# Products as two column tiles of 64 on TensorE: scores, values, denominators and MLP of an attention and MLP kernel

## The chip, the cores and the metric

One Trainium2 chip, one of its cores. The time is the device time of one launch in microseconds, median of several runs; lower is better. The kernel before took 470.49 us (three runs, 470.36 to 472.8).

PE is TensorE, which multiplies; PEld is the part of it that loads weights. ACT is ScalarE, DVE is VectorE, POOL is GpSimd, SP is SyncE, which issues DMAs.

## The reference

Attention with a relative position bias over 8 batches, 8 heads, 576 positions and 64 columns a head, followed by an MLP over the 4608 rows of 512 columns that the attention leaves:

```
scores = q @ k.T / sqrt(64) + bias[bucket(|i - j|), head]
attn   = softmax(scores)
x      = (attn @ v), heads beside one another      # 4608 x 512
h      = x @ w_in                                   # 4608 x 2048
g      = h + sin(alpha * h)**2 / (alpha + 1e-9)
out    = g @ w_out                                  # 4608 x 512
```

Inputs and output are float32; the products are computed in float16 with sums in float32.

## The kernel before, in words

The eight batches t are worked one after another, and each is an attention stage and an MLP-in stage. In an attention stage four head pairs p follow one another; the two heads of a pair are z = 0 and 1. The 576 queries are cut into two windows of 384 and 192 columns (`WIN`).

- **Scores** (`plan_pair`, `qk`, L565): keys x queries. The tile `kz` holds the keys of each head beside 64 zero rows, so that one 128-row product gives the scores of one head. A window of 384 takes nine products, one to a PSUM buffer `sc`; one of 192 also takes nine, all but one of them two to a buffer. ACT turns each buffer into exponentials in `u` (L572), DVE multiplies those near the diagonal by the bias factor (L605, L588).
- **av** (`plan_av`, L631 and L637): for each window two tasks, y = 0 the denominators (weights are ones) and y = 1 the values (weights are v). A task is nine matmuls into one PSUM buffer `av`: first L631 for the last 64 keys of both heads with 128-column weights (`ones2` or `vh`), then L637 eight times with 64-column weights, head 0 to output rows 0 to 63 and head 1 to rows 64 to 127. ACT makes the reciprocal of the denominators (Ln at L653, Exp at L657), and DVE multiplies it in and writes the MLP's input `xT` (L668).
- **MLP-in** (`plan_moe_in`, L693): 512 rows of x to a block, 16 blocks of 128 hidden columns f, four products of 512 columns each into an `sc` buffer; ACT takes the sine (L700), ACT or DVE the square (L707, L709), DVE adds (L714) into the tile `g`.
- **MLP-out** (`plan_mo`, L741): for each 128 rows, 16 products of 512 columns into a `mo` buffer, copied out by DVE or ACT (L473, L471). There are nine blocks: 4608 rows of 512; the last batch has two of them.
- **Start**: `warm` (L388) issues products on zeros; q and k of batches 0 and 1 are turned by transposes on PE (L486, L493), into `mo` buffers that ACT and DVE copy. From batch 2 on, DMA transposes do it.

The order on each engine is not written by hand. Every piece of work is a task with dependencies, a priority and a guessed duration; `Plan.run` simulates the four engines and emits at each step the task that can start first (ties within 0.02 us by priority). MLP-out products are fill: they have the lowest priority, so they go where PE would otherwise stand still, and during the scores of a batch no more than `OFFSET + QUOTA * share` of them are taken. av tasks carry the mark `tiled`, and where the mark of a PE task differs from that of the one before, the planner adds `D_MODE` (0.115 us) to its start. Two `g` tiles are in use in turn, so the MLP-in of block 8 needs the MLP-out of block 6 done.

Of the kernel before, what the change touches and what calls it, by code (L numbers as in the profile page):

```python
# [152 lines left out]


WINDOW = 700
D_MODE = 0.115
WARM_END = 40.0
FILL_GAP = 0.0
QUOTA = 48
# [28 lines left out]
def kernel(  # L188
# [11 lines left out]
    nc = tc.nc  # L200
# [8 lines left out]
    NF = FF // 128  # L209
# [4 lines left out]
    XN = 1536  # L214
# [21 lines left out]
    kzs = [sgl.tile([128, NP, 2 * S], F16, name=f"kz{i}") for i in range(2)]  # L236
# [18 lines left out]
    zz = sgl.tile([128, 512], F16, name="zz")  # L255
# [125 lines left out]
    def clear_v(eng, i):  # L381
        eng.memset(vhs[i][0:64, :, 1, :], 0.0)
        eng.memset(vhs[i][64:128, :, 0, :], 0.0)

    def warm(n):
        x = new_mo()
        for _ in range(n):
            nc.tensor.matmul(out=x, lhsT=zz[:, 0:128], rhs=zz, start=True, stop=True)  # L388

    def cast0(kq, j, eng):  # L390
        n = SN[2 * j]
# [147 lines left out]
    def plan_pair(t, p, kqt, first, gate, ub, band_nb):  # L539

        u = Cell()
        done = {}
        units, head = [], []
        for w in range(2):
            units += [(w, 4, 0)]
            for c in range(0, 4, 1 + w):
                units += [(w, c, 0), (w, c, 1)]
        for i, (w, c, z) in enumerate(units):
            q0, n = WIN[w]
            nc_ = 1 if w == 0 or c == 4 else 2  # L550
            b, sc = Buf("sc"), Cell()

            def qk(e, i=i, w=w, c=c, z=z, q0=q0, n=n, nc_=nc_, sc=sc):
                if i == 0:
                    if p == 0:
                        first()
                        plan.in_qk, plan.used = True, 0
                    u.v = new_u()
                plan.share = (len(units) * p + i + 1) / (NP * len(units))
                if p == NP - 1 and i == len(units) - 1:  # L560
                    plan.in_qk = False
                sc.v = new_sc()
                for y in range(nc_):
                    k0 = 512 if c == 4 else (128 * (c + y), S + 64 + 128 * (c + y))[z]
                    nc.tensor.matmul(  # L565
                        out=sc.v[:, n * y : n * y + n], lhsT=kzs[t % 2][:, p, k0 : k0 + 128],
                        rhs=qTs[t % 2][:, p, q0 : q0 + n], start=True, stop=True,
                    )

            def ex(e, w=w, c=c, z=z, q0=q0, n=n, nc_=nc_, sc=sc):  # L570
                k0 = 8 if c == 4 else 4 * z + c
                nc.scalar.activation(  # L572
                    out=u.v[:, k0 : k0 + nc_, q0 : q0 + n], in_=sc.v[:, 0 : n * nc_],
                    func=AF.Exp, scale=0.125,
                )

            base = PB + 100 * (16 * p + i)
            m = plan.add({"PE": nc_ * t_pe(n)}, qk, kqt, base, after=head, new=[b] + ([ub] if i == 0 else []))
            head = head or [m]
            x = plan.add({"ACT": t_act(n * nc_)}, ex, [m] + gate, base + 20, use=[b, ub])  # L580
            if c == 4:
                if w == 0:
                    done[(w, 4, 0)] = done[(w, 4, 1)] = x
                    continue

                def bh(e):
                    io = u.v[:, 8, 384:576]
                    nc.vector.tensor_tensor(out=io, in0=io, in1=mh[:, p, 0:192], op=ALU.mult)  # L588

                x = plan.add({"DVE": 0.17}, bh, [x] + mh_tasks, base + 10, nb=band_nb, use=[ub])  # L590
                done[(w, 4, 0)] = done[(w, 4, 1)] = x
                continue
            for y in range(nc_):
                done[(w, c + y, z)] = x
            if z == 0:
                continue
            for cc in range(c, c + nc_):
                lo, hi = max(q0, 128 * cc - 128), min(q0 + n, 128 * cc + 256)
                if lo >= hi:
                    continue  # L600

                def bd(e, cc=cc, lo=lo, hi=hi):
                    io = u.v[:, 0:8, lo:hi].rearrange("p (z c) q -> p z c q", z=2)[:, :, cc]
                    x0 = lo - 128 * cc + 128
                    nc.vector.tensor_tensor(  # L605
                        out=io, in0=io, in1=m2[:, 2 * p : 2 * p + 2, x0 : x0 + hi - lo],
                        op=ALU.mult,
                    )

                x = plan.add({"DVE": 0.07 + (hi - lo) / 960.0}, bd,  # L610
                             [done[(w, cc, 0)], done[(w, cc, 1)]], base + 10, nb=band_nb,
                             use=[ub])
                done[(w, cc, 0)] = done[(w, cc, 1)] = x
        return u, done
# [3 lines left out]
    def plan_av(t, p, w, u, ub, done):  # L618

        q0, n = WIN[w]  # L620
        lb, rb = Buf("ln"), Buf("rd")
        bs, avs = [Buf("av"), Buf("av")], [Cell(), Cell()]
        ln, rd = Cell(), Cell()
        base = PB + 100 * (16 * p + 8 * w + 8)
        us = [done[(w, c, z)] for c in range(5) for z in range(2)]
        prev = av_last
        for y in range(2):

            def mm(e, y=y):
                o = avs[y].v = new_av()  # L630
                nc.tensor.matmul(  # L631
                    out=o[:, 0:n], lhsT=vhs[t % 2][:, p] if y else ones2,
                    rhs=u.v[:, 8, q0 : q0 + n], start=True, stop=False,
                )
                for c in range(4):
                    for z in range(2):
                        nc.tensor.matmul(  # L637
                            out=o[64 * z : 64 * z + 64, 0:n],
                            lhsT=vs[t % 2][:, c, 2 * p + z, :] if y else ones,
                            rhs=u.v[:, 4 * z + c, q0 : q0 + n],  # L640
                            start=False, stop=(c == 3),
                        )

            prev = [plan.add({"PE": 5 * t_pe(n)}, mm, us + prev[:], base + AV_PRI + y,
                             nb=T_V0 if t == 0 and y else 0.0, new=[bs[y]], use=[ub])]
            prev[0].tiled = True
            if y:
                av_last[:] = prev
                continue

            def lg(e):
                ln.v = new_ln()
                nc.scalar.activation(out=ln.v[:, 0:n], in_=avs[0].v[:, 0:n], func=AF.Ln)  # L653

            def rc(e):
                rd.v = new_rd()
                nc.scalar.activation(  # L657
                    out=rd.v[:, 0:n], in_=ln.v[:, 0:n], func=AF.Exp, scale=-1.0
                )

            l_ = plan.add({"ACT": t_act(n)}, lg, prev, base + LN_PRI, new=[lb], use=[bs[0]])
            r = plan.add({"ACT": t_act(n) + 0.04}, rc, [l_], base + LN_PRI, new=[rb], use=[lb])

        def ml(e):
            x0 = (S * t + q0) % XN
            for a, m in ((0, min(n, XN - x0)), (min(n, XN - x0), n)):
                if a < m:
                    nc.vector.tensor_tensor(  # L668
                        out=xT[:, p, (x0 + a) % XN : (x0 + a) % XN + m - a],
                        in0=avs[1].v[:, a:m], in1=rd.v[:, a:m], op=ALU.mult,  # L670
                    )

        return r, [plan.add({"DVE": t_dve(n)}, ml, av_last[:] + [r], base - 300,
                            use=[bs[1], rb])]
# [5 lines left out]
    def plan_moe_in(b, tbl):  # L680
# [5 lines left out]
        for f in range(NF):  # L686
# [3 lines left out]
            def mm(e, f=f, h=h):  # L690
                h.v = new_sc()
                for j in range(4):
                    nc.tensor.matmul(  # L693
                        out=h.v, lhsT=w_in16[:, j, 128 * f : 128 * f + 128],
                        rhs=xT[:, j, 512 * b % XN : 512 * b % XN + 512], start=(j == 0), stop=(j == 3),
                    )

            def sn(e, f=f, h=h, s16=s16):
# [34 lines left out]
    def plan_mo(b, a):  # L733

        mb, ob, m = Buf("mo"), Buf("outs"), Cell()
        for f in range(NF):

            def mm(e, f=f):
                if f == 0:
                    m.v = new_mo()  # L740
                nc.tensor.matmul(  # L741
                    out=m.v, lhsT=gcell[b].v[:, f, 128 * a : 128 * a + 128],
                    rhs=w_out16[:, f, :], start=(f == 0), stop=(f == NF - 1),
                )

            mo_last[:] = [plan.add({"PE": t_pe(512)}, mm, mo_last[:] + [gdone[(b, f)]],
                                   500000000 + 4 * b + a, nb=T_WO if b == 0 else 0.0, new=[mb] if f == 0 else [],
                                   use=[gbuf[b]] if f == 0 else [gbuf[b], mb])]
            mo_last[0].fill = True
# [88 lines left out]
```

## Time and profile before

| | |
|---|---|
| three runs, us | 470.49 median (470.36, 470.49, 472.8) |
| the profiled execution, us | 473.36 |
| its span, first to last instruction, us | 471.6 |
| its granted PE clock, mean | 0.993 |
| matmuls on PE | 3073 |
| ACT busy, share of the span | 81% |

The page gives for each engine the time in which at least one instruction of it was running, then the same in 40 slices of the span (a 9 is 90% or more), then groups of instructions by line. A group's row has the count, the busy time, the mean duration of one, and the idle time ahead of it with its cause. A timeline row has the start, the length from first start to last end, and the instructions that it merges. Matmul rows overlap: the next one starts before the one ahead has ended, so the distance between starts is what a product costs, and the duration is not. PEclk is the share of the full clock that PE was granted.

### The profile page before, as it was taken

What the parts mean: (1) busy time and instruction counts of PE and PEld (TensorE: products, weight loads), DVE (VectorE), ACT (ScalarE), POOL (GpSimd) and SP (SyncE); (2) the same over time, 40 slices, a digit from 0 to 9 for tenths busy, and PEclk for the clock granted to TensorE, in tenths of its full rate; (3) what the DMA queues carried; (4) which work ended last, traced back from release to release, by engine and by line L of the source; (5) the groups of instructions that cost most, each with busy time, mean ns of one, the idle gap of its engine ahead of it and who ended that gap; (6) DMA issues with size and microseconds to landing.
All of it is one profiled execution on the core that took longest, in us unless ns stands there. A gap on an engine that the chain in (4) does not pass through costs nothing.

```text
span 471.6 us, 8180 instructions
## 1 busy us (share of the span) xinstructions
PE 452.2 (96%) x3073; PEld 225.6 (48%) x3073; DVE 269.2 (57%) x565; ACT 383.4 (81%) x834; POOL 91.1 (19%) x104
## 2 busy tenths in 40 slices
PE   5688899999999999999999999999999999999996
PEld 2344444554455445554455445544555455544442
DVE  3745496446844585449544764568544954489600
ACT  2769799869988799779987998879887998799611
POOL 7669640007000420025000700040000000000000
PEclk9989899999999999999999999999999999999999
DMA  9699999409900996049901990094101000100021
GB/s 132 172 218 180 185 158 178 87 26 180 159 28 24 117 168 62 24 101 161 108 24 46 177 147 22 24 143 81 46 1 44 2 23 24 46 1 1 22 90 67
DMA packets 144935, 41.28 MB, mean 88 GB/s; under 512 B 132424, under 2 KB 139776, under 8 KB 144896
## 3 DMA queue, kind: packets, MB, share of 16 engines
q0 software_dynamic: 94720, 16.88, 45.2%
q1 hardware_dynamic: 49360, 23.52, 21.8%
q10 hardware_dynamic: 816, 0.36, 0.3%
q8 instruction: 24, 0.39, 0.3%
q14 instruction: 15, 0.12, 0.1%
HBM read 37.56 MB, written 16.52 MB: 115 GB/s over the span
## 4 chain that ended last, share of the span: by engine, by line
PE 60%; ACT 23%; DMA 8%; issue 5%; POOL 2%; DVE 2%; ACTq 0%; POOLq 0%; DVEq 0%
PE mo L741 21%; PE av L637 15%; PE sc L565 12%; PE sc L693 6%; PE av L631 5%; ACT L762 4%; DMA nat_95<-in_q_dram 3%; ACT sq L707 3%; ACT u L572 2%; DMA w_in_79<-in_moe_w_in_dram 2%; DMA w_out_80<-e_dram 1%; POOL m_77 L446 1%; DVE g L714 1%; DMA tabL<-in_bias_table_dram 1%; DMA e_dram<-e_sb 1%
## 5 line engine op out<-in xcount | busy, mean ns | idle before, releaser
L572 ACT ACTIVATE u<-sc 128x384 f16<-128x384 f32 x448 | 173.0, 545 | 3.9 <-PE sc L565 3.8
L741 PE MATMUL mo<-w_out_80,g 128*128 128x512 f16 x576 | 173.5, 379 | 0.0
L693 PE MATMUL sc<-xT,w_in_79 128*128 128x512 f16 x576 | 130.5, 379 | 0.3 <-DVE g L714 0.3
L605 DVE TENSOR_TENSOR u<-u,m_77 128x512 f16<-128x512 f16 (+1 forms) x192 | 73.8, 402 | 73.6 <-ACT u L572 72.0
L714 DVE SCALAR_TENSOR_TENSOR g<-sq,inv_a,sc 128x512 f16<-128x512 f16 x144 | 104.6, 747 | 3.6 <-ACT sq L707 0.6
L693 PEld LDWEIGHTS <-w_in_79 128*128 128x128 f16 x576 | 55.5, 98 | 66.9 <-issue 0.6
L741 PEld LDWEIGHTS <-g 128*128 128x128 f16 x576 | 55.6, 97 | 53.3 <-issue 4.1
L565 PE MATMUL sc<-qT_70,kz_67 128*128 128x384 f16 (+1 forms) x288 | 63.7, 285 | 0.2
L565 PE MATMUL sc<-qT_69,kz_66 128*128 128x384 f16 (+1 forms) x288 | 62.1, 288 | 1.5 <-ACT u L572 0.3
L653 ACT ACTIVATE lnd<-av 128x384 f32<-128x384 f32 x64 | 27.1, 423 | 43.8 <-PE av L637 43.8
L668 DVE TENSOR_TENSOR xT<-av,rd 128x384 f16<-128x384 f32 (+1 forms) x68 | 29.5, 438 | 55.4 <-ACT rd L657 32.5
L637 PE MATMUL av<-u,ones 128*64 128x192 f16 (+1 forms) x512 | 44.2, 295 | 0.0
L565 PEld LDWEIGHTS <-kz_66 128*128 128x128 f16 x288 | 25.9, 98 | 22.1 <-issue 6.1
L565 PEld LDWEIGHTS <-kz_67 128*128 128x128 f16 x288 | 26.7, 97 | 19.8 <-issue 0.8
L335 POOL DMA_DIRECT2D v_72<-in_v_dram x12 | 10.6, 894 | 122.2 <-PE av L637 122.2
L473 DVE COPY outs<-mo 128x512 f32<-128x512 f32 x28 | 19.3, 688 | 18.3 <-PE mo L741 18.3
L657 ACT ACTIVATE rd<-lnd 128x384 f32<-128x384 f32 x64 | 28.3, 442 | 1.2
L637 PEld LDWEIGHTS <-ones 128*64 128x64 f16 x512 | 21.8, 110 | 13.8 <-issue 7.8
L335 POOL DMA_DIRECT2D v_71<-in_v_dram x12 | 10.6, 894 | 86.2 <-PE av L637 86.2
L637 PE MATMUL av<-u,v_71 128*64 128x384 f16 (+1 forms) x256 | 23.1, 304 | 0.0
L637 PE MATMUL av<-u,v_72 128*64 128x384 f16 (+1 forms) x256 | 21.8, 292 | 0.0
L471 ACT ACTIVATE outs<-mo 128x512 f32<-128x512 f32 x8 | 4.8, 597 | 20.6 <-PE mo L741 20.6
(361 smaller groups left out, 396.8 us busy)
## 6 DMA issues: line engine op xcount, KB each, us to landing
out_dram<-outs SPq DMA_DIRECT2D x36, 256.0 KB, 2.0
staged_k<-in_k_dram POOLq DMA_DIRECT2D x6, 576.0 KB, 13.8
staged_q<-in_q_dram POOLq DMA_DIRECT2D x6, 576.0 KB, 15.4
w_out_80<-in_v_dram SPq DMA_DIRECT2D x8, 256.0 KB, 4.3
w_in_79<-in_moe_w_in_dram POOLq DMA_DIRECT2D x4, 512.0 KB, 10.1
w_out_80<-in_moe_w_out_dram POOLq DMA_DIRECT2D x4, 512.0 KB, 10.6
v_71<-in_v_dram POOLq DMA_DIRECT2D x12, 128.0 KB, 4.4
v_72<-in_v_dram POOLq DMA_DIRECT2D x12, 128.0 KB, 4.5
```

The source lines that it names most:

```text
L335: nc.gpsimd.dma_start(out=vs[t % 2][:, c], in_=vp[128 * c : 128 * c + 128],)
L565: nc.tensor.matmul(out=sc.v[:, n * y : n * y + n], lhsT=kzs[t % 2][:, p, k0 : k0 + 128], rhs=qTs[t % 2][:, p, q0 : q0 + n], start=True, st ...
L572: nc.scalar.activation(out=u.v[:, k0 : k0 + nc_, q0 : q0 + n], in_=sc.v[:, 0 : n * nc_], func=AF.Exp, scale=0.125,)
L605: nc.vector.tensor_tensor(out=io, in0=io, in1=m2[:, 2 * p : 2 * p + 2, x0 : x0 + hi - lo], op=ALU.mult,)
L631: nc.tensor.matmul(out=o[:, 0:n], lhsT=vhs[t % 2][:, p] if y else ones2, rhs=u.v[:, 8, q0 : q0 + n], start=True, stop=False,)
L637: nc.tensor.matmul(out=o[64 * z : 64 * z + 64, 0:n], lhsT=vs[t % 2][:, c, 2 * p + z, :] if y else ones, rhs=u.v[:, 4 * z + c, q0 : q0 + n] ...
L653: nc.scalar.activation(out=ln.v[:, 0:n], in_=avs[0].v[:, 0:n], func=AF.Ln)
L657: nc.scalar.activation(out=rd.v[:, 0:n], in_=ln.v[:, 0:n], func=AF.Exp, scale=-1.0)
L668: nc.vector.tensor_tensor(out=xT[:, p, (x0 + a) % XN : (x0 + a) % XN + m - a], in0=avs[1].v[:, a:m], in1=rd.v[:, a:m], op=ALU.mult,)
L693: nc.tensor.matmul(out=h.v, lhsT=w_in16[:, j, 128 * f : 128 * f + 128], rhs=xT[:, j, 512 * b % XN : 512 * b % XN + 512], start=(j == 0), s ...
L714: nc.vector.scalar_tensor_tensor(out=gcell[b].v[:, f, :], in0=sq.v, scalar=inv_a[:, f : f + 1], in1=h.v, op0=ALU.mult, op1=ALU.add,)
L741: nc.tensor.matmul(out=m.v, lhsT=gcell[b].v[:, f, 128 * a : 128 * a + 128], rhs=w_out16[:, f, :], start=(f == 0), stop=(f == NF - 1),)
```

## The change

A helper `mm2` issues each product as two matmuls, one for weight columns 0 to 63 into output rows 0 to 63, and one for columns 64 to 127 into rows 64 to 127, both with the same moving operand. It is used for the warm-up, the scores, the first product of each av task, and both MLP products. The transposes stay, and so does the small product for the bias table. What is computed is the same. The planner's `D_MODE` becomes 0.

```diff
-D_MODE = 0.115
+D_MODE = 0.0
...
+    def mm2(out, lhsT, rhs, start, stop):
+
+        for z in range(2):
+            nc.tensor.matmul(
+                out=out[64 * z : 64 * z + 64], lhsT=lhsT[:, 64 * z : 64 * z + 64], rhs=rhs,
+                start=start, stop=stop,
+            )
+
     def warm(n):
         x = new_mo()
         for _ in range(n):
-            nc.tensor.matmul(out=x, lhsT=zz[:, 0:128], rhs=zz, start=True, stop=True)
+            mm2(x, zz[:, 0:128], zz, True, True)
...
-                    nc.tensor.matmul(
-                        out=sc.v[:, n * y : n * y + n], lhsT=kzs[t % 2][:, p, k0 : k0 + 128],
-                        rhs=qTs[t % 2][:, p, q0 : q0 + n], start=True, stop=True,
+                    mm2(
+                        sc.v[:, n * y : n * y + n], kzs[t % 2][:, p, k0 : k0 + 128],
+                        qTs[t % 2][:, p, q0 : q0 + n], True, True,
                     )
...
-                nc.tensor.matmul(
-                    out=o[:, 0:n], lhsT=vhs[t % 2][:, p] if y else ones2,
-                    rhs=u.v[:, 8, q0 : q0 + n], start=True, stop=False,
+                mm2(
+                    o[:, 0:n],
+                    (vhs[t % 2][:, p] if y else ones2).rearrange("p z d -> p (z d)"),
+                    u.v[:, 8, q0 : q0 + n], True, False,
                 )
...
-                    nc.tensor.matmul(
-                        out=h.v, lhsT=w_in16[:, j, 128 * f : 128 * f + 128],
-                        rhs=xT[:, j, 512 * b % XN : 512 * b % XN + 512], start=(j == 0), stop=(j == 3),
+                    mm2(
+                        h.v, w_in16[:, j, 128 * f : 128 * f + 128],
+                        xT[:, j, 512 * b % XN : 512 * b % XN + 512], j == 0, j == 3,
                     )
...
-                nc.tensor.matmul(
-                    out=m.v, lhsT=gcell[b].v[:, f, 128 * a : 128 * a + 128],
-                    rhs=w_out16[:, f, :], start=(f == 0), stop=(f == NF - 1),
+                mm2(
+                    m.v, gcell[b].v[:, f, 128 * a : 128 * a + 128], w_out16[:, f, :],
+                    f == 0, f == NF - 1,
                 )
```

PE's instructions go from 3073 loads and 3073 matmuls to 4940 each. In the new kernel every one that `mm2` issues has the line of the helper, L388, and L637 is L646, L493 is L501. With `D_MODE` at 0 the planner also sets another order. The 128 av tasks stood in 37 unbroken runs on PE and now stand in 91, most of them one or two tasks with scores between. An attention stage of batches 1 to 7 had 61 to 64 MLP-out products and has 50 to 52; an MLP-in stage had 3 and has 3 to 5; behind the start of the last MLP-in block there were 125 and are 187.

The first place is on PE in the first attention stage with MLP-out products (batch 1), where the first denominators begin; a row is the line, the instruction, output<-inputs and output size. Before:

```order
L741 LDWEIGHTS g
L741 MATMUL mo<-w_out_80,g 128x512
L565 LDWEIGHTS kz_67
L565 MATMUL sc<-qT_70,kz_67 128x384
L631 LDWEIGHTS ones_76
L631 MATMUL av<-u,ones_76 128x384
L637 LDWEIGHTS ones
L637 MATMUL av<-u,ones 64x384
```

and now:

```order
L388 LDWEIGHTS kz_67
L388 MATMUL sc<-qT_70,kz_67 64x192
L388 LDWEIGHTS ones_76
L388 MATMUL av<-u,ones_76 64x384
L388 LDWEIGHTS ones_76
L388 MATMUL av<-u,ones_76 64x384
L646 LDWEIGHTS ones
L646 MATMUL av<-u,ones 64x384
```

The 128-row outputs are gone: scores, the first product of the task and the rest all have 64 rows. The task also comes earlier, behind the last scores of its own head pair instead of behind the first seven of the next.

The second place is on PE at the end of the attention stage of batch 0, around the transposes (of `nat_95`, batch 1's q and k). Before, they follow the last scores, and the last head pair's av tasks follow the second group of twelve:

```order
L565 LDWEIGHTS kz_66
L565 MATMUL sc<-qT_69,kz_66 128x192
L493 LDWEIGHTS nat_95
L493 MATMUL mo<-id_sb,nat_95 64x128
L493 LDWEIGHTS nat_95
L493 MATMUL mo<-id_sb,nat_95 64x128
```

```order
L493 LDWEIGHTS nat_95
L493 MATMUL mo<-id_sb,nat_95 64x32
L631 LDWEIGHTS ones_76
L631 MATMUL av<-u,ones_76 128x384
L637 LDWEIGHTS ones
L637 MATMUL av<-u,ones 64x384
```

and now the first transposes follow the values of the long window:

```order
L646 LDWEIGHTS v_71
L646 MATMUL av<-u,v_71 64x384
L646 LDWEIGHTS v_71
L646 MATMUL av<-u,v_71 64x384
L501 LDWEIGHTS nat_95
L501 MATMUL mo<-id_sb,nat_95 64x128
```

Both av tasks of 384 columns have moved ahead of the transposes; the two of 192 columns now stand behind twelve and behind twenty-four of them.

## The prediction

> **What bounds the kernel now.** I read the busy shares first, then the slices, then stretches of one batch, then single rows.
>
> ```profile
> PE 452.2 (96%) x3073; PEld 225.6 (48%) x3073; DVE 269.2 (57%) x565; ACT 383.4 (81%) x834; POOL 91.1 (19%) x104
> PE   5688899999999999999999999999999999999996
> PEclk9989899999999999999999999999999999999999
> ```
>
> PE is full from the sixth slice on, at its full clock; the first five slices (59 us) are not. Batches 1 to 6 repeat: one stretch from table load to table load, then batch 3 cut into its attention stage and its MLP-in stage.
>
> ```profile
> 175.08:225.71 50.63, 50.48 (x345) 25.60 (x344) 30.06 (x65) 44.36 (x98) 9.24 (x8) 1.00 0.81 92
> 327.06:377.69 50.63, 50.48 (x345) 25.60 (x344) 30.07 (x65) 44.36 (x98) 0.00 (x0) 1.00 0.06 22
> 175.08:208.80 33.72, 33.66 (x261) 17.83 (x259) 15.87 (x41) 27.99 (x71) 0.00 (x0) 1.00 0.40 54
> 208.80:225.71 16.91, 16.82 (x88) 7.77 (x85) 14.19 (x25) 16.38 (x27) 9.24 (x8) 1.00 1.62 166
> ```
>
> Columns: window, its length, busy PE, PEld, DVE, ACT, POOL, granted clock, DMA, GB/s. PE is busy 50.48 of 50.63 us, ACT 44.36. But a matmul row lasts longer than its turn, so busy is not work; the turn is the distance between starts:
>
> ```profile
> 201.33 0.33 PE L565 MATMUL sc<-qT_70,kz_67 128*128 128x384 f16 x1
> 201.49 0.38 PE L741 MATMUL mo<-w_out_80,g 128*128 128x512 f16 x1
> 201.71 0.33 PE L565 MATMUL sc<-qT_70,kz_67 128*128 128x384 f16 x1
> ...
> 202.84 0.25 PE L565 MATMUL sc<-qT_70,kz_67 128*128 128x192 f16 x1
> 202.93 0.38 PE L741 MATMUL mo<-w_out_80,g 128*128 128x512 f16 x1
> ...
> 441.43 26.28 PE L741 MATMUL mo<-w_out_80,g 128*128 128x512 f16 x121
> ```
>
> The 121 products at the end step by (26.28 - 0.38) / 120 = 0.216 us at 512 columns. 384 and 192 columns by proportion give 0.162 and 0.081; the rows show 0.16 and 0.09. Now the av tasks (denominators with ones, values with v):
>
> ```profile
> 188.75 0.34 PE L631 MATMUL av<-u,ones_76 128*128 128x384 f16 x1
> 189.02 0.84 PE L637 MATMUL av<-u,ones 128*64 128x384 f16 x8
> 189.79 0.34 PE L631 MATMUL av<-u,vh_74 128*128 128x384 f16 x1
> 190.06 0.84 PE L637 MATMUL av<-u,v_72 128*64 128x384 f16 x8
> 190.83 0.26 PE L631 MATMUL av<-u,ones_76 128*128 128x192 f16 x1
> 191.02 0.52 PE L637 MATMUL av<-u,ones 128*64 128x192 f16 x8
> 191.47 0.82 PE L565 MATMUL sc<-qT_70,kz_67 128*128 128x384 f16 x4
> ```
>
> A task is one 128-wide product and four pairs of 64-wide ones. Long: 189.79 - 188.75 = 1.04 us where five turns are 0.81. Short: 191.47 - 190.83 = 0.64 where five are 0.41. The excess is 0.23 either way. It splits alike too: 0.11 between the wide product and the first pair (0.27 - 0.16; 0.19 - 0.08), 0.12 over the four pairs (0.77 - 0.65; 0.45 - 0.33). An excess that doesn't grow with the columns is a fixed price of going from wide to narrow and back. The Trainium skill, "TensorEngine Tiling (Array Packing)", Key Properties, says that a change of tiling mode drains the engine; these rows agree.
>
> A whole batch is then 128 MLP products x 0.216 = 27.6, 36 + 36 score products 8.7, sixteen av tasks of five turns 9.7, together 46.0; with 16 x 0.23 = 3.7 it is 49.7 of the 50.63 measured. So 0.9 us a batch is real waiting, and **PE's turns set the time** from batch 1 on.
>
> **The change, part by part.** *The switches.* Everything in batches 1 to 7 becomes 64-wide, so the 0.23 goes 7 x 16 = 112 times. I take 0.225 for rounding: **-25.2 us**. The profiled execution took 473.36 us and PE's span is 471.6; the three runs have a median of 470.49. I sum in differences and apply them to the median, 2.87 below the profiled one.
>
> *The pairs in place of wide products.* 576 score, 128 av, 576 + 576 MLP products: 1856 new pairs. What a new pair costs beyond the old product is not shown at 512, but pairs at 384 and 192 bound it. Of the 0.12 over four pairs the way back to wide should take what the way in takes, 0.11; that leaves 0.01 / 4 = 0.0025 us a pair. If the way back were free it would be 0.03. A pair below the old turn is excluded, since each half streams all columns. I take 0, the nearest to equal ways in and out: **0 us**; ends 0 and +4.6 (1856 x 0.0025), with 0.03 kept for a rival.
>
> ```profile
> L741 PEld LDWEIGHTS <-g 128*128 128x128 f16 x576 | 55.6, 97 | 53.3 <-issue 4.1
> L637 PEld LDWEIGHTS <-ones 128*64 128x64 f16 x512 | 21.8, 110 | 13.8 <-issue 7.8
> ```
>
> A load of half the columns lasts longer, 110 against 97 ns, and there will be two. The eight loads of a short run sum to 0.88 us and the run steps in 0.45, so they lie beside one another and beside products; the cover is the previous pair, and 512 columns give more of it than 192. One rule of the Trainium skill speaks against this change: "TensorE: Matmul & The Clock Gate", Part 3, The mechanism, says that a weight load overlaps running matmuls only where the row group differs, and column tiles share theirs. By that rule no load of a pair would be hidden; the 0.45 us of this trace disagrees with it. If the rule held here all the same, the sum would be that of the third rival below.
>
> *The start.* In batch 0 PE waits for data, and there the order counts:
>
> ```profile
> 45.66 0.58 PE L493 MATMUL mo<-id_sb,nat_95 128*64 128x128 f16 x12
> 46.48 0.30 PE L493 MATMUL mo<-id_sb,nat_95 128*64 128x128 f16 x4 [0.25 <-DMA nat_95<-in_q_dram]
> 47.99 0.58 PE L493 MATMUL mo<-id_sb,nat_95 128*64 128x128 f16 x8 [1.20 <-DMA nat_95<-in_q_dram]
> 48.50 0.44 PE L631 MATMUL av<-u,ones_76 128*128 128x384 f16 x1
> ...
> 50.30 0.50 PE L631 MATMUL av<-u,vh_73 128*128 128x384 f16 x1
> ...
> 52.11 0.26 PE L631 MATMUL av<-u,ones_76 128*128 128x192 f16 x1
> ...
> 55.54 5.35 PE L693 MATMUL sc<-xT,w_in_79 128*128 128x512 f16 x24
> 45.00:50.00 5.00, 3.44 (x39) 1.72 (x36) 1.71 (x5) 3.52 (x9) 5.00 (x5) 0.86 1.14 154
> 50.00:55.00 5.00, 4.35 (x55) 2.24 (x51) 2.20 (x4) 3.09 (x6) 1.56 (x2) 0.80 1.22 201
> ```
>
> 24 transposes of batch 1 stand ahead of the last av tasks, and their data lands at about 48. The two long av tasks then cost 52.11 - 48.50 = 3.6 us, slowed by a clock of 0.86 and 0.80. In the changed order they stand ahead of the transposes, where PE otherwise waits. The gain is at most 3.6 plus the switches of the two short tasks, 0.45; it is nothing if MLP-in 0 starts by another clock. I take **-3.0**, since the first product of MLP-in follows these rows directly; ends 0 and -5. The other batch 0 switches lie beside ACT's exps and the loads and count nothing; without that cover they would be 12 x 0.225 = 2.7, of which the end of -5 has a part.
>
> *What is late next.* With the holes of PE gone, ACT is close. The program order has 50 to 52 output products (L741) in an attention stage instead of 61 to 64, and 187 behind the last batch's second MLP-in start instead of 125. This moves work, and PE loses none by it. But the attention stage becomes 33.72 - 3.6 - 10 x 0.216 = 28.0 us of PE, and ACT is busy 27.99 in it. ACT's real need is a little less, as rows overlap there:
>
> ```profile
> L572 ACT ACTIVATE u<-sc 128x384 f16<-128x384 f32 x448 | 173.0, 545 | 3.9 <-PE sc L565 3.8
> 176.37 1.65 ACT u L572 x4
> ACT lnd L653 <- PE av L637: 5.8, 7, 1.8
> ```
>
> Four exps step by (1.65 - 0.545) / 3 = 0.37 (0.545 is the mean of the first row). The third row, from the waits of this batch, says that ACT stood 5.8 us for av results, which the shorter av tasks also cut. Two engines in program order with the same load trade small waits. Bounds: 0 (all in holes) and 3.0 a batch (half the 5.8 kept on top of 27.99). I take 0.6, near the 0.9 that PE waits now: 7 x 0.6 = **+4.2 us**. The tail (row 441.43) is unchanged: PE alone, 0.216 a product.
>
> Sum: -25.2 + 0 - 3.0 + 4.2 = -24.0. That is 449.4 in the profiled execution's terms and **446.5 us** against the median.
>
> **The rivals.** *ACT takes over* (463 us): the waits of ACT for av stay by half, an attention stage becomes 27.99 + 2.9 = 30.9 instead of 28.0, and 7 x 3.0 = 21 replaces 4.2, which adds 16.8. For it: the equal loads, and a plan whose holes are now all filled. Against: ACT's rows overlap, and it waits for av tasks that get shorter. Anything between 455 and 463 belongs here.
>
> *Pairs cost more than products* (511 us, the slower side): the way back is free and each pair pays 0.03 for its two longer loads. Then only the entries go, 112 x 0.11 = 12.3, and 470.5 - 12.3 - 3.0 + 1856 x 0.03 (55.7) = 511. It decides from 24.0 / 1856 = 13 ns a pair. For it: 110 against 97 ns, twice as many loads, and no pair of 512 columns in this trace. Against: the excess is 0.12 for short and long runs alike, though a short one has half the cover.
>
> *No load is hidden* (651 us): each pair stands for one load of 0.110 us before it streams, and 1856 x 0.110 = 204 comes on top of 446.5. Against: eight such loads, 0.88 us, fit into 0.45. This is what the rule on row groups in the Trainium skill ("TensorE: Matmul & The Clock Gate", Part 3, The mechanism) would do.
>
> *The change does not do what it says* (470 us): the 0.23 comes with each av task for another reason, such as its first weights, and stays. Then only the start moves, and its ends are 0 and -3. Against: the price is the same with ones and with v, going in and coming out.
>
> **How the numbers follow.** Forecast 0.74 (446.5, own range 438.5 to 455), ACT takes over 0.16, no effect 0.04, dearer pairs 0.05, loads not hidden 0.01. Downward: -5 at the start and no new waiting give 446.5 - 2 - 4.2 = 440.3, and the 0.9 a batch that waits now may shrink by some; I end at 438.5. Upward 459 takes dear pairs by 0.0025 (+4.6) and half of the ACT case (+8), and leaves the slower cases out. Faster by over 0.5% (2.35 us, about what a measurement of this kernel can tell from no change): 0.74 + 0.16 = 0.90; within it 0.04; slower 0.05 + 0.01 = 0.06.
>
> **What would show it.** In the profile after, an av task of five pairs of 384 columns should step in 0.81 us and one of 192 in 0.41, without a gap to its neighbours; the products at the end should still step by 0.216 (0.23 or more there is the pair rival). A batch should take 50.63 - 3.6 + 0.6 = 47.6 us, less 1.9 for nine output products that move to the end, so 45.7, with PE waiting 1.5 of them; 48 with waits between PE and ACT is the ACT rival. MLP-in 0 should start at about 52.5 instead of 55.54, and 187 output products should stand around and behind the last MLP-in. Wrong would be a granted clock below 1.00 in batches 1 to 7, or av tasks that keep 1.04.

## The result, and the profile after

The changed kernel takes **447.21 us** (four runs, 445.36 to 447.94) against 471.03 for the kernel before: a ratio of 0.9483, 95% interval 0.9442 to 0.9523. The profiled execution took 446.98 us with a span of 445.2; that of before took 473.36 and 471.6. The busy shares, and PE and its clock in 40 slices, on the page of after:

```profile
PE 426.2 (96%) x4940; PEld 302.8 (68%) x4940; DVE 261.9 (59%) x555; ACT 385.3 (87%) x844; POOL 91.0 (20%) x104
PE   5879999999999999999999999999999999999996
PEclk9999999999999999999999999999999999999999
```

PE has 60% more instructions and is busy 26 us less; ACT's busy time is nearly the same (385.3 against 383.4 us). The granted clock is 0.9 or more in every slice. Batch 3 of after by windows, whole and then its attention and its MLP-in stage, with the columns of the prediction:

```profile
160.58:206.10 45.52, 45.13 (x546) 33.73 (x543) 28.83 (x62) 44.46 (x100) 9.23 (x8) 1.00 0.92 84
160.58:189.35 28.77, 28.38 (x390) 22.62 (x387) 15.06 (x39) 28.13 (x73) 0.00 (x0) 1.00 0.42 51
189.35:206.10 16.75, 16.75 (x160) 11.11 (x157) 13.77 (x24) 16.33 (x27) 9.23 (x8) 1.00 1.78 140
```

A batch has gone from 50.63 to 45.52 us, attention from 33.72 to 28.77. In this window PE issues 119 products of 512 columns, 76 of 384 and 76 of 192 (a pair counted as one), at the prediction's 0.216, 0.162 and 0.081 us a total of 44.2. So 1.3 us is not product time; before it was 50.63 - 46.1 = 4.5, switches included. I call this the **rest** of a batch below. In batches 1 to 6 of after it lies between 0.9 and 1.4. The av tasks of that batch, on PE's timeline of after:

```profile
166.47 0.35 PE L388 MATMUL av<-u,ones_76 128*64 128x384 f16 x2
166.63 0.84 PE L646 MATMUL av<-u,ones 128*64 128x384 f16 x8
167.28 0.36 PE L388 MATMUL av<-u,vh_74 128*64 128x384 f16 x2
...
168.42 0.28 PE L388 MATMUL av<-u,ones_76 128*64 128x192 f16 x2
168.50 0.52 PE L646 MATMUL av<-u,ones 128*64 128x192 f16 x8
168.83 0.68 PE L388 MATMUL sc<-qT_70,kz_67 128*64 128x384 f16 x6
```

A long task steps in 167.28 - 166.47 = 0.81 us (1.04 before), a short one in 168.83 - 168.42 = 0.41 (0.64 before). The 0.23 is gone from both. What the loads show, from the groups of after:

```profile
L646 PEld LDWEIGHTS <-ones 128*64 128x64 f16 x512 | 30.5, 110 | 4.2
```

The same loads as before, 110 ns each, without the 7.8 us of "issue" that stood ahead of them, which fits loads that are not taken ahead across a change of width. The end, by the chain of waits, first of before, then of after:

```profile
441.59 26.13 PE mo L741 x121
...
390.75 13.60 PE mo L388 x126
415.18 26.13 PE mo L388 x242
```

242 halves take the 26.1 us that 121 whole products took. A pair of 512 columns costs what the product cost. The 63 products at 390.75 are those that moved there from the batches.

The start, on PE's timeline of after, then the same windows as in the prediction, and what waited in MLP-in 0:

```profile
43.90 0.36 PE L388 MATMUL av<-u,ones_76 128*64 128x384 f16 x2
...
45.52 0.58 PE L501 MATMUL mo<-id_sb,nat_95 128*64 128x128 f16 x12
...
47.81 0.60 PE L501 MATMUL mo<-id_sb,nat_95 128*64 128x128 f16 x8 [1.00 <-DMA nat_95<-in_q_dram]
...
49.81 5.37 PE L388 MATMUL sc<-xT,w_in_79 128*64 128x512 f16 x48
45.00:50.00 5.00, 3.94 (x80) 3.01 (x77) 3.52 (x8) 3.74 (x7) 5.00 (x6) 1.00 1.22 150
50.00:55.00 5.00, 5.00 (x48) 2.71 (x46) 3.79 (x7) 4.62 (x9) 5.00 (x6) 1.00 1.19 196
```

```profile
PE sc L388 <- DVE g L723: 1.8, 4, 0.7
```

The long av tasks lie ahead of the transposes, and MLP-in 0 starts at 49.81 instead of 55.54. Inside it PE then stands 1.8 us for DVE, which has batch 1's copies to make as well; batch 1's table load comes at 69.9 instead of 73.2. Not all of this is the order: from 45 to 55 us PE was granted 0.86 and 0.80 of its clock in the profile of before and all of it in this one. The two long av tasks took 3.6 us there, with 0.46 of switches in them, and take 45.52 - 43.90 = 1.6 here. The clock accounts for about the rest: 0.14 and 0.20 of 5 us each are 1.7 us.

### The profile page after: what moved, and what is told of

Same layout as the page of the kernel before. It is cut to its first block, busy times and chain, and to the rows that moved or that the text cites. A ratio compares the mean times of both kernels' runs of the same rounds, so it can differ in the third digit from the quotient of the medians.

```text
span 445.2 us, 12071 instructions
## 1 busy us (share of the span) xinstructions
PE 426.2 (96%) x4940; PEld 302.8 (68%) x4940; DVE 261.9 (59%) x555; ACT 385.3 (87%) x844; POOL 91.0 (20%) x104
## 3 DMA queue, kind: packets, MB, share of 16 engines
q1 hardware_dynamic: 49360, 23.52, 25.2%
## 4 chain that ended last, share of the span: by engine, by line
PE 72%; DMA 10%; ACT 10%; DVE 2%; issue 2%; POOL 2%; SPq 1%; ACTq 0%; POOLq 0%; DVEq 0%
PE sc L388 32%; PE mo L388 25%; PE av L646 12%; PE av L388 3%; DMA nat_95<-in_q_dram 3%; DMA w_in_79<-in_moe_w_in_dram 2%; DMA qT_69<-staged_q 2%; ACT L771 2%; ACT sq L716 2%; DVE g L723 1%; DMA w_out_80<-e_dram 1%; DMA tabL<-in_bias_table_dram 1%; POOL m_77 L454 1%; DMA e_dram<-e_sb 1%; ACT u L580 1%
## 5 line engine op out<-in xcount | busy, mean ns | idle before, releaser
L388 PE MATMUL mo<-w_out_80,g 128*64 128x512 f16 x1152 | 172.1, 379 | 0.0
L388 PE MATMUL sc<-xT,w_in_79 128*64 128x512 f16 x1152 | 132.6, 379 | 1.0 <-DVE g L723 1.0
L723 DVE SCALAR_TENSOR_TENSOR g<-sq,inv_a,sc 128x512 f16<-128x512 f16 x144 | 102.2, 744 | 23.9 <-PE mo L388 12.3
L388 PEld LDWEIGHTS <-w_in_79 128*64 128x64 f16 x1152 | 78.0, 110 | 45.4 <-DVE g L723 2.0
L388 PEld LDWEIGHTS <-g 128*64 128x64 f16 x1152 | 79.3, 110 | 22.0
L388 PE MATMUL sc<-qT_70,kz_67 128*64 128x384 f16 (+1 forms) x576 | 68.0, 287 | 2.0 <-ACT u L580 1.1
L388 PE MATMUL sc<-qT_69,kz_66 128*64 128x384 f16 (+1 forms) x576 | 67.1, 292 | 2.3 <-ACT u L580 1.3
L388 PEld LDWEIGHTS <-kz_67 128*64 128x64 f16 x576 | 43.0, 108 | 20.5 <-issue 5.3
L388 PEld LDWEIGHTS <-kz_66 128*64 128x64 f16 x576 | 40.6, 109 | 20.6 <-issue 9.3
L646 PE MATMUL av<-u,ones 128*64 128x192 f16 (+1 forms) x512 | 43.9, 286 | 0.0
L479 ACT ACTIVATE outs<-mo 128x512 f32<-128x512 f32 x15 | 8.9, 595 | 30.7 <-PE mo L388 30.7
L646 PEld LDWEIGHTS <-ones 128*64 128x64 f16 x512 | 30.5, 110 | 4.2
L662 ACT ACTIVATE lnd<-av 128x384 f32<-128x384 f32 x64 | 29.3, 458 | 3.4 <-PE av L646 2.9
L646 PE MATMUL av<-u,v_71 128*64 128x384 f16 (+1 forms) x256 | 22.1, 286 | 0.0
L646 PE MATMUL av<-u,v_72 128*64 128x384 f16 (+1 forms) x256 | 21.8, 286 | 0.0
L388 PE MATMUL av<-u,ones_76 128*64 128x192 f16 (+1 forms) x128 | 20.4, 286 | 0.0
```

Of the source, the lines that this page charges most:

```text
L388: nc.tensor.matmul(out=out[64 * z : 64 * z + 64], lhsT=lhsT[:, 64 * z : 64 * z + 64], rhs=rhs, start=start, stop=stop,)
L479: nc.scalar.activation(out=o, in_=i, func=AF.Copy)
L646: nc.tensor.matmul(out=o[64 * z : 64 * z + 64, 0:n], lhsT=vs[t % 2][:, c, 2 * p + z, :] if y else ones, rhs=u.v[:, 4 * z + c, q0 : q0 + n] ...
L723: nc.vector.scalar_tensor_tensor(out=gcell[b].v[:, f, :], in0=sq.v, scalar=inv_a[:, f : f + 1], in1=h.v, op0=ALU.mult, op1=ALU.add,)
```

## The experiments

The change is two things, narrow products and another order. The first four runs take them apart and vary how many changes of width there are. The kernel before was timed anew beside each group of runs: its median was 471.81 us beside these four, 472.13 beside the shorter reciprocal and the two runs on the start, 473.17 beside the other buffers. So 1 or 2 us between runs of different groups are not shown by the times alone, and there I go by the length of a batch.

**Pairs in the order of before.**

```diff
-D_MODE = 0.0
+D_MODE = 0.115
```

> The changed kernel with D_MODE back at 0.115, so the order of before with every product in pairs. PE then has 6 changes of column width instead of 274. Theory (a fixed price of about 0.11 us for each change of width, whatever instruction stands there): the 25 us of batches 1 to 7 go, the 3 us of the start stay, so 447 to 451 us, a batch of 46 to 47 us, and MLP-in 0 still starting near 55. Rival 'the order did it': near 470. Rival 'a price of the av task itself': near 470 too.

Measured: 454.66 us (ratio 0.9633, 0.9597 to 0.9669). The rivals fall, and MLP-in 0 starts at 54.02, near 55 as expected, but the time misses the expectation by 4 us: a batch takes 48.16 instead of 46 to 47, with a rest of 2.0 us. Where it is, on PE's timeline of this run at the end of batch 3's attention stage:

```profile
197.32 0.36 PE L388 MATMUL av<-u,ones 128*64 128x384 f16 x2
197.48 0.84 PE L646 MATMUL av<-u,ones 128*64 128x384 f16 x8
198.45 0.35 PE L388 MATMUL av<-u,vh 128*64 128x384 f16 x2
198.61 0.84 PE L646 MATMUL av<-u,v 128*64 128x384 f16 x8
199.26 0.28 PE L388 MATMUL av<-u,ones 128*64 128x192 f16 x2
199.34 0.53 PE L646 MATMUL av<-u,ones 128*64 128x192 f16 x8
200.17 0.27 PE L388 MATMUL av<-u,vh 128*64 128x192 f16 x2 [0.30 <-DVE xT L677]
...
200.58 1.71 PE L388 MATMUL sc<-xT,w_in 128*64 128x512 f16 x14
```

The first long task steps in 1.13 us instead of 0.81, the short one in 0.91 instead of 0.41: 0.32 and 0.50 us of waiting, the second for DVE's multiply, which empties the av buffer. Four av tasks follow one another here, and there are two buffers. The same four in before:

```profile
206.17 0.34 PE L631 MATMUL av<-u,ones_76 128*128 128x384 f16 x1
...
208.25 0.26 PE L631 MATMUL av<-u,ones_76 128*128 128x192 f16 x1
...
209.04 0.24 PE L631 MATMUL av<-u,vh_74 128*128 128x192 f16 x1
...
209.67 1.68 PE L693 MATMUL sc<-xT,w_in_79 128*128 128x512 f16 x7
```

They took 209.67 - 206.17 = 3.50 us and take 200.58 - 197.32 = 3.26 now. Four times 0.23 is gone from them, 0.92 us, and only 0.24 is gained: waits stand where the switches were. The same place in after:

```profile
185.91 0.35 PE L388 MATMUL av<-u,ones_76 128*64 128x384 f16 x2
...
187.53 0.63 PE L388 MATMUL mo<-w_out_80,g 128*64 128x512 f16 x4
187.97 0.28 PE L388 MATMUL av<-u,ones_76 128*64 128x192 f16 x2
188.05 0.53 PE L646 MATMUL av<-u,ones 128*64 128x192 f16 x8
188.38 0.63 PE L388 MATMUL mo<-w_out_80,g 128*64 128x512 f16 x4
188.81 0.28 PE L388 MATMUL av<-u,vh_74 128*64 128x192 f16 x2
```

Two output products stand in each gap: PE does work there and waits for nothing.

**The new order with the products of before.**

```diff
-D_MODE = 0.115
+D_MODE = 0.0
```

> The kernel before with D_MODE at 0, so the new order with the wide products kept. PE has 274 changes of width, as before. Theory: the price stays, only the start can gain, so 466 to 471 us, and an av task of five products of 384 columns still steps in 1.04 us. Rival 'the order did it': 447 to 455.

Measured: 470.88 us (ratio 0.9977, 0.9951 to 1.0003), a gain that can't be told from none. On PE's timeline of this run the price is where it was:

```profile
173.26 0.32 PE L631 MATMUL av<-u,ones 128*128 128x384 f16 x1
173.52 0.84 PE L637 MATMUL av<-u,ones 128*64 128x384 f16 x8
174.29 0.34 PE L631 MATMUL av<-u,vh 128*128 128x384 f16 x1
```

1.03 us a long task, and a rest of 4.7 us a batch. So the order alone gives about 1 us and the pairs alone 17 (medians of this group), while both give 24.

**Only the first product of an av task as a pair.** The kernel before with `mm2` in `plan_av` alone.

```diff
-                nc.tensor.matmul(
-                    out=o[:, 0:n], lhsT=vhs[t % 2][:, p] if y else ones2,
-                    rhs=u.v[:, 8, q0 : q0 + n], start=True, stop=False,
+                mm2(
+                    o[:, 0:n],
+                    (vhs[t % 2][:, p] if y else ones2).rearrange("p z d -> p (z d)"),
+                    u.v[:, 8, q0 : q0 + n], True, False,
                 )
```

> The kernel before with only the first product of each av task as a pair, D_MODE at 0.115. The scores and both MLP products stay wide. As the av tasks stand in few unbroken runs, PE has 88 changes of width instead of 274. Theory (price by the number of changes): 186 x 0.112 = 20.8 us less, about 450 us (447 to 453); tasks inside a run step in 0.81 us, and only the first and last of a run pay. Rival 'a price of the av task itself' (its first weights, its wait): it is paid 128 times as before, 468 to 471. Rival 'pairs cost more at 512 columns': this one would then beat the full change, as it has none there.

Measured: 457.3 us (ratio 0.9685, 0.965 to 0.972). This small edit, with about 90 changes of width left, brings most of what all pairs bring in that order (454.66), so the price goes with the changes and not with the av task. It doesn't beat the full change either, as it would if pairs of 512 columns were dearer. The size was missed by 7 us, as in the first run: the rest is 2.4 us a batch, only 0.4 above that run although eight more changes a batch are made. That fits changes that lie where PE would wait anyway; no row here shows it.

**MLP-out wide in the changed kernel.**

```diff
-                mm2(
-                    m.v, gcell[b].v[:, f, 128 * a : 128 * a + 128], w_out16[:, f, :],
-                    f == 0, f == NF - 1,
+                nc.tensor.matmul(
+                    out=m.v, lhsT=gcell[b].v[:, f, 128 * a : 128 * a + 128],
+                    rhs=w_out16[:, f, :], start=(f == 0), stop=(f == NF - 1),
                 )
```

> The changed kernel with only the MLP-out product wide again, in the same order. These products stand one by one between scores, so PE has 571 changes of width instead of 6, and no more wide products than before. Theory: 565 x 0.11 = 62 us more, about 509 us where PE sets the time everywhere, and not under 490; slower than before. Rival 'a price of the av task itself': 447, as the av tasks are those of the changed kernel. Rival 'it is the wide product's own time': at most the time before.

Measured: 502.96 us (ratio 1.0656, 1.0611 to 1.0701), 6 under the 509 expected. PE's timeline of this run:

```profile
196.29 0.39 PE L750 MATMUL mo<-w_out,g 128*128 128x512 f16 x1
196.61 0.35 PE L388 MATMUL sc<-qT,kz 128*64 128x384 f16 x2
196.90 0.39 PE L750 MATMUL mo<-w_out,g 128*128 128x512 f16 x1
```

A product of 512 and a pair of 384 step in 0.61 us where the turns are 0.38: 0.32 instead of 0.216, and 0.29 instead of 0.162. Each direction costs 0.10 to 0.13, on products that have nothing to do with av. Over the span it is 501.2 - 445.2 = 56.0 us for 565 changes, 0.099 each.

**A shorter way to the reciprocal, in the old order and in the new.** The first is the first run of the experiments with this edit, the second the changed kernel with it.

```diff
-                nc.scalar.activation(out=ln.v[:, 0:n], in_=avs[0].v[:, 0:n], func=AF.Ln)
+                nc.scalar.activation(
+                    out=ln.v[:, 0:n], in_=avs[0].v[:, 0:n], func=AF.Copy, scale=3.0e-6
+                )
...
-                rd.v = new_rd()
-                nc.scalar.activation(
-                    out=rd.v[:, 0:n], in_=ln.v[:, 0:n], func=AF.Exp, scale=-1.0
-                )
+                rd.v = ln.v
```

> The order of before with every product in pairs (the first run of this study), and one scaled copy on ACT in place of the Ln and the Exp of the denominators; the true reciprocal is left out, so the output is not the reference's. ACT loses about 2.6 us of steps a batch, and the way from denominators to the freed av buffer gets shorter by 0.4 to 0.5 us. Theory (in the old order the last head pair's four av tasks stand behind one another, have two buffers, and wait for this way, 0.31 + 0.50 us a batch, where the switches used to lie): these two waits go, PE waits about 1.1 us a batch instead of 1.96, and the time is 448 to 450 instead of 454.7. Rival 'PE waits there for exps': under 2 us gained.

Measured: 452.88 us (ratio 0.9582, 0.9548 to 0.9616), 1.8 less instead of 5 to 7; a batch takes 47.78 us instead of 48.16, and the rest goes from 2.0 to 1.7. My theory was mostly wrong. In batch 3 the first long task still steps in 1.04 us (1.13 in the first run), and the short one in 0.91, as there. The rival's number fits, but not its cause, for this is what the last short task waits for, by PE's, DVE's and ACT's timelines:

```profile
198.15 0.27 PE L388 MATMUL av<-u,vh 128*64 128x192 f16 x2 [0.30 <-DVE xT L676]
```

```profile
197.54 0.56 DVE L676 TENSOR_TENSOR xT<-av,lnd 128x384 f16<-128x384 f32 x1 [1.16 <-PE av L646]
```

```profile
196.43 0.49 ACT L662 ACTIVATE lnd<-av 128x384 f32<-128x384 f32 x1 [1.51 <-PE av L646]
```

The reciprocal is there by 196.92, and DVE starts the multiply that empties the buffer at 197.54, when PE's values are: the values themselves hold the buffer, not the reciprocal. Where most of the 0.4 us a batch came from, these rows don't show.

> The same edit in the changed kernel, with the same part left out. There MLP-out products stand between the last av tasks, and the 1.1 us that PE waits a batch are scores waiting for exps. Theory: the shorter way from denominators to buffer brings nothing by itself; ACT's 2.6 us a batch bring at most half of the 1.1, so 443.5 to 446.5 (0.5 to 3.5 us less), a smaller gain than in the old order. Rival 'ACT bounds the batches': the batch shortens by 2 us or more with more output products left to the end, and PE's wait falls under 0.3 us a batch, 439 to 441.

Measured: 445.24 us (ratio 0.9419, 0.9387 to 0.9451), 2.0 less than the changed kernel by the medians, but the runs of the two overlap (444.66 to 446.7, and 445.36 to 447.94). Batch 3 of this run by windows:

```profile
161.64:206.91 45.27, 44.88 (x546) 33.77 (x543) 28.89 (x62) 41.67 (x92) 9.24 (x8) 1.00 0.95 88
```

ACT is busy 41.67 us instead of 44.46, and the batch is 0.25 us shorter. ACT, though busy 98% of a batch of after, does not bound it: the rival asked for 2 us a batch. In this profile the clock fell to 0.67 between 50 and 55 us, and the first 24 products of MLP-in 0 took 6.9 us instead of 5.2. The order around them is that of after, and 0.33 of 5 us is 1.65 us, so the clock alone can move a start by that much.

**Other buffers for the last values, in the old order and in the new.** Again the first run and the changed kernel.

```diff
-                o = avs[y].v = new_av()
+                o = avs[y].v = new_sc() if y and p == NP - 1 else new_av()
```

> The order of before with every product in pairs (first run of this study), and the two value tasks of the last head pair of each batch write into score buffers, which are free there, in place of the two av buffers. All work and its order stay. Theory (in the old order the last av tasks wait for an av buffer that DVE's multiply has to empty): the waits of 0.31 and 0.50 us at the end of each attention stage go, PE waits about 1.1 to 1.3 us a batch instead of 1.96, and the time is 448.5 to 451 instead of 454.7 us. Rival 'these tasks wait for exps or their bias factors': nothing changes, 454 to 456.

Measured: 453.2 us (ratio 0.9584, 0.9556 to 0.9612), 1.5 less instead of 4 to 6. On PE's timeline of this run:

```profile
197.08 0.36 PE L388 MATMUL av<-u,ones 128*64 128x384 f16 x2
...
197.89 0.36 PE L388 MATMUL sc<-u,vh 128*64 128x384 f16 x2
...
198.70 0.28 PE L388 MATMUL av<-u,ones 128*64 128x192 f16 x2
...
199.12 0.28 PE L388 MATMUL sc<-u,vh 128*64 128x192 f16 x2
...
199.53 3.65 PE L388 MATMUL sc<-xT,w_in 128*64 128x512 f16 x32
203.43 1.92 PE L388 MATMUL sc<-xT,w_in 128*64 128x512 f16 x16 [0.26 <-DVE g L723]
```

What these tasks wait for in the old order is shown: with other buffers they step in 0.81, 0.81 and 0.42, and both waits at the stage's end are gone. But a batch gets only 0.33 us shorter (47.83), for about half of what they took returns in MLP-in as a wait for DVE: the 16 products from 199.53 take 3.90 us until the next one, where 16 turns are 3.46. A wait that was taken away with no work put in its place moved on. The new order puts output products there, and its batches are shorter; that these products are the whole reason is argued, not shown.

> The same edit in the changed kernel, where output products stand between the last av tasks. Theory: no wait for an av buffer is left there, so nothing changes: 446 to 448 us. Rival 'two av buffers hold up the new order as well': 444 or less.

Measured: 447.73 us (ratio 0.9466, 0.9434 to 0.9499), as the changed kernel: on PE no av task waits for DVE to empty a buffer there.

**The start: transposes earlier, and loads earlier.** The changed kernel, first with the first edit alone, then with both.

```diff
-T_TR1 = 36.0
+T_TR1 = 30.0
...
-    load_w_in16()
     for kq, src in ((0, k), (1, q)):
         load_nat(nat2, kq, 0, H, src[1], nc.gpsimd)
+    load_w_in16()
```

> The changed kernel with T_TR1 at 30 and the loads as they were: most of batch 1's transposes stand ahead of the last head pair's scores and av tasks, though their data lands at 45 to 48. Theory of the start (what stands behind these transposes on PE waits with them): PE stands from about 41 to 46 and MLP-in 0 starts 3 us or more later than 49.8, as before the change; 449 to 453 us. Rival 'MLP-in 0 sets the start, not the order ahead of it': within 1 us of the changed kernel, 446 to 448.

Measured: 450.5 us (ratio 0.9528, 0.9496 to 0.956). PE's timeline of this run:

```profile
42.81 0.30 PE L501 MATMUL mo<-id_sb,nat 128*64 128x128 f16 x4 [0.84 <-DMA nat<-in_k_dram]
...
57.37 1.49 PE L388 MATMUL sc<-xT,w_in 128*64 128x512 f16 x12
```

PE waits at the transposes, and scores and av tasks wait behind them; MLP-in 0 starts at 57.37 instead of 49.81. What stands behind the transposes on PE does wait with them. Part of the 7.6 us is again the clock, 0.65 and 0.67 from 45 to 55 us, by the same estimate up to 3.4 us. Batch 1's table load is 4.7 us later (74.65).

> The changed kernel with the loads of q and k of batch 1 ahead of those of w_in on POOL's queue, and T_TR1 at 30, which puts most of batch 1's transposes ahead of the last head pair's scores. Theory of the start (transposes of batch 1 wait for their data until 47.8 us, and their copies crowd MLP-in 0, where PE waits 2.2 us for DVE): the data lands at about 40, MLP-in 0 starts by 50 as now, carries half the copies, and batch 1 starts 2 to 4 us earlier: 443 to 445 us. Rival 'w_in becomes what is waited for': it lands at about 48 or later, MLP-in 0 starts late, 447 to 450.

Measured: **444.34 us** (ratio 0.9403, 0.9372 to 0.9435), 2.9 less than the changed kernel and the fastest of all; its four runs (443.32 to 445.25) lie below all four of the changed kernel. Its MLP-in 0 starts later than expected, at 51.38, but PE waits 0.2 us in it for DVE instead of 1.8, and batch 1's table load is at 68.7 instead of 69.9.

## Why the prediction was right, step by step

The predicted time was 446.5 us, a gain of 24.0; measured are 447.21 and 23.8. Two errors of about 2 us with opposite signs, told below, make it so close; that part is luck. The two profiled executions differ by 26.4, because that of before lay 2.9 above its median.

- **PE's turns set the time, and 0.23 us a task goes: right.** The tasks step in 0.81 and 0.41. With the order held (the new order with wide products against the changed kernel) the medians differ by 23.7 us and the spans by 23.4, of the 25.2 put down. A batch takes 45.52 us (45.7 was predicted).
- **A pair costs what the product cost: right.** 26.13 us for 121 pairs at the end, as for 121 products. The dearer pairs and the loads not hidden are ruled out. The rule of the Trainium skill ("TensorE: Matmul & The Clock Gate", Part 3, The mechanism) that a weight load overlaps only matmuls of another row group does not hold for these column tiles: the loads of both halves take all 128 rows, and the products step as before. The 121 wide products at the end of before, with loads of 97 ns on the same rows, had already stepped in 0.216 us. The same section of the Trainium skill also lets a load go ahead that targets a background weight buffer; no run here shows whether that is what happened.
- **New waits between PE and ACT, +4.2: too large.** 25.2 - 23.4 leaves 1.8 us. In the same order the rest of a batch goes from 4.7 to 1.3, so 3.4 of the 3.6 that sixteen switches cost. ACT stayed out of the way although both engines are full in an attention stage (28.38 and 28.13 us of 28.77): taking 2.8 us a batch from ACT gained 0.25 of it.
- **The start, -3.0: the mechanism right in part, the size too large.** By the profiled pair the new order alone moves batch 1 from 73.2 to 70.2, the 3.0 put down. By the medians of that run it is 0.9, with an interval from 2.3 down to nothing. MLP-in 0 came 5.7 us earlier, more than predicted; the copies on DVE, which I had not priced, took part of it back. I had also counted the lower clock of the profile of before as the order's: of the 3.6 us of its two long av tasks, 1.6 is clock, for at full clock, with the same wide products in the new order, they take 2.0. How much of the start is order and how much clock, no run separates. The error here is some 2 us and the one above 2.4, of opposite signs.
- **"This moves work, and PE loses none by it": incomplete.** I credited the order with the start alone. With pairs it is worth 454.66 - 447.21 = 7.5 us. In the profiled pair 1.7 of them lie ahead of batch 1's table load (71.64 and 69.91), the others in the batches. In the old order a part of the switches lay where the last av tasks would have waited for a buffer (0.92 us of price in those of batch 3, 0.24 gained), so that without switches 17 us and not 24 are gained. The sum was right because the change has both halves; the account of what each does was not.
- **The rivals.** No effect fell with the result and with the run that has only the new order, where the price is still there. ACT takes over fell with the result and with the shorter reciprocal. The prediction gives its upper end as 455 and also works out 459; the result lies under both.

What stays open: why PE's last 1.3 us a batch are waited, beyond the few rows at scores that name ACT.

## What to carry to other kernels

Where an engine is full, take the distance between starts and not the duration as the cost of a product, and compare each mix of neighbours with the pure sequence: an excess that doesn't grow with size points to a price of the change between two kinds. Vary the number of changes to show it; here it went when all products had one kind, even with 60% more instructions. A price that is paid where something else would wait is worth less than its count; multiply by the changes only after looking at what the next instruction would wait for. Here an order that puts independent work into such places brought the rest, and by itself it showed no clear gain. Look at the granted clock before you credit a stage's gain to the order.

## What the runs showed of the hardware

- A change between 128-column and 64-column products costs PE 0.10 to 0.13 us in either direction, for 192, 384 and 512 columns alike, where PE would not wait anyway, and 565 of them cost 56 us.
- Twice the weight loads, each longer (110 against 97 ns), cost nothing at 192, 384 and 512 columns: pairs step in 0.081 to 0.083, 0.162 and 0.216 us.
- Transposes with 64-column outputs go with the pairs: they stand between MLP-in products in the changed kernel without an excess (24 products from 49.81 to the next transpose at 55.02 are 24 x 0.217; before, 24 from 55.54 to the transpose at 60.82 took 0.07 us more). The way back costs less here: from that transpose to the next product it is 0.51 us before (60.82 to 61.33) and 0.48 after (55.02 to 55.50).
- The granted clock fell between 45 and 55 us, to 0.65 to 0.86 in at least one of the two windows, in the profiles of before, of its order in pairs, of the av pairs alone, of the old order with the shorter reciprocal and with other buffers, and of the early transposes. In the other profiles, all of them of the new order, it was full there, except in that of the shorter reciprocal (0.67). No run shows what sets it.
